# V of the first three quads loaded in two transfers, their PV evicted in two copies, and two FFN1 products placed behind the third PV

## The chip, the cores and the metric

The kernel runs on one core of one Trainium2 chip. The metric is the time of one execution on the device, in microseconds. All kernels here are one program for one core, with the inputs in HBM as float32 and the output as float32.

## What is computed

A sigmoid attention is followed by a SwiGLU feed-forward block without residuals or norms. The attention has 8 batches, 12 heads, sequence length 448 and head dimension 64; the block takes the 3584 tokens of 768 features that come out of it, with 1536 hidden features.

```python
scores = scale * np.matmul(q, k.transpose(0, 1, 3, 2)) - np.log(S)   # scale = 1/sqrt(64)
attn = 1.0 / (1.0 + np.exp(-scores))
attn_out = np.matmul(attn, v)                                        # (8, 12, 448, 64)
x = attn_out.transpose(0, 2, 1, 3).reshape(B * S, H * D)             # (3584, 768)
g = x @ w_gate
silu = g * (1.0 / (1.0 + np.exp(-g)))
out = (silu * (x @ w_val)) @ w_out                                   # (3584, 768)
```

## The kernel before

**Units of work.** The heads are taken in quads: quad `n` is the four heads `4j` to `4j+3` of batch `b`, with `n = 3b + j`, so there are 24. The 448 keys of a quad are cut into 7 chunks of 64; chunk `c` of quad `n` is written (n,c) below. For each chunk, `qk_tile` (L246) makes the scores of the four heads with four matmuls of 64 rows and 64 columns of the array (L254). They go into one PSUM tile of two banks: `h2` is the bank, and within a bank one head lies on partitions 0 to 63 and another on 64 to 127. `sig_tile` (L263) turns the tile into probabilities with one ScalarE activation of 128x896 (L273), or in two halves (L270). When the 7 chunks are there, `pv` (L276) accumulates the products with V in another PSUM tile, with 28 matmuls of 64x64 (L289), and evicts it into two SBUF tiles `xT` of 128 partitions: the features of two heads each, which is the layout that the feed-forward part reads. `trans_pe` (L235) transposes q and k of a quad on TensorE (L223, copied out by DVE at L229); later quads are transposed by DMA (L211).

**Which head lies where.** A matmul of 64 rows in the upper half of the array can write partitions of the lower half. The function `flip(n)` (L186) chooses between two layouts. Without the flip, V arrives in one transfer of 128 partitions (L197), and PV leaves the heads of bank 1 with the two partition halves exchanged, so the second eviction is two copies of 64 partitions each (L313 on DVE; for `how=2` at L311 on ScalarE), each to the other half. With the flip, V arrives in two transfers of 64 partitions (L195), which put heads 0 and 3 on one half and heads 1 and 2 on the other, the scores of the second bank are written to exchanged halves (`g` at L253), and the second eviction is one copy of 128 partitions. In the kernel before, quads 0 to 4 are not flipped and quads 5 to 23 are.

**PSUM.** All eight banks are a ring of four two-bank tiles (`ring`, L72). `Banked` (L79) takes the next tile, or the one named with `at`. A tile can be written again when its last readers are done. Thus QK waits for the sigmoid that read the tile four places earlier, and PV and the first products of FFN1 wait in the same way for their tiles.

**The order of the work.** Each engine works through its own list of instructions in order. For the first 30 us this list is written out by hand (L811 to L945): loads and casts, the chunks of quads 0, 1 and 2, their PV, and between them the transposes of the next quad and the first products of FFN1 for batch 0. In this stretch the tiles go round so that `pv(1)` takes the tile of `pv(0)`, and `early[0]`, the first FFN1 tile, takes that of `pv(1)`. From L964 on a planner mixes the attention of later quads into the feed-forward work by due times.

**FFN1.** For hidden block `f` (128 features) of batch `b`, `ffn1_mm` (L325) accumulates x times the gate weights in bank 0 and x times the value weights in bank 1, over six blocks `pr` of 128 features of x (L330). Block `pr` needs tile `xT` of quad `pr // 2`. So the first four products of a bank can run when quads 0 and 1 are evicted; products 4 and 5 wait for quad 2. In the hand-written part the first three hidden blocks (`early[0]` to `early[2]`) are begun with the first four products, around the last chunks and the PV of quad 2, and then finished.

**Queues.** q and k of quads 0 to 3 are issued by SyncE (SP; one part of quad 0's q by ScalarE), in the kernel's first microseconds. V, the weights and q and k of quads 4 to 6 are issued by GpSimd (POOL), in the order V0, V1, first gate and value weights (`wg`, `wv`), V2, second `wg` and `wv`, q and k of quad 4, q and k of quad 5, third `wg` and `wv`, V3. Each of these transfers also converts to 16 bits, except those of q and k. A POOL transfer waits at its issue for the landing of the eighth POOL transfer before it.

Of the kernel before, what the change touches and what calls it, by code (L numbers as in the profile page):

```python
# [20 lines left out]
def kernel(  # L21
# [95 lines left out]
    def apart(second, *firsts):  # L117

        for first in firsts:
            keys[0] += 1  # L120
            tc.add_to_no_dep_group(f"half{keys[0]}", first.ins)
            tc.declare_no_dep(second.ins, group=f"half{keys[0]}", reason="another bank or other partitions")
# [25 lines left out]
    def half_of(a):  # L148
        return a.rearrange("p a b s -> p (a b s)").bitcast(FP16)
# [34 lines left out]
        qkv_st[(n, which)] = st  # L184

    def flip(n):  # L186
        return n > 4

    def load_v(n):
        t = v16p.tile([128, 2, S], FP16, tag="v16", name=f"v16_{n}")  # L190
        if flip(n):
            b, j = divmod(n, NJ)
            src = v[b, 4 * j:4 * j + 4].rearrange("h (p c) d -> p h (c d)", c=C)
            for w, heads in enumerate((slice(0, 4, 3), slice(1, 3))):
                nc.gpsimd.dma_start(out=t[w * 64:(w + 1) * 64], in_=src[:, heads])  # L195
        else:
            nc.gpsimd.dma_start(out=t, in_=src_of(n, 2))  # L197
        v16[n] = t
# [47 lines left out]
    def qk_tile(n, c, at=None):  # L246
        sd = Banked(at=at)
        sc = sd.t
        qt, kt = qT[(n, 0)], qT[(n, 1, c)]
        for w in range(2):  # L250
            for h2 in range(2):
                r = slice(h2 * 64, h2 * 64 + 64)
                g = (w ^ (h2 and flip(n))) * 64  # L253
                nc.tensor.matmul(  # L254
                    out=sc[g:g + 64, h2, :S],
                    lhsT=kt[r, w * 64:(w + 1) * 64],
                    rhs=qt[r, :, w * 64:(w + 1) * 64],
                    start=True,
                    stop=True,
                )  # L260
        return sd
# [14 lines left out]
    def pv(n, how=0, at=None, then=None):  # L276

        b, j = divmod(n, NJ)
        P = Banked(at=at).t
        vt = v16.pop(n)  # L280
        for c in range(C):
            pt = pts.pop((n, c))
            for h2 in range(2):
                for w in range(2):
                    r, g = w * 64, (w ^ h2) * 64
                    if flip(n):
                        r, g = g, r
                    r = slice(r, r + 64)
                    nc.tensor.matmul(  # L289
                        out=P[g:g + 64, h2, :S],  # L290
                        lhsT=vt[r, h2, c * D:(c + 1) * D],
                        rhs=pt[r, h2, :],
                        start=(c == 0),
                        stop=(c == C - 1),
                    )

        def x_tile(h2):
            if n >= NQ - NJ:
                at = 4 * W2 + (2 * j + h2) * S
                return half_of(stg_a)[:, at:at + S]  # L300
            return xtp.tile([128, S], FP16, tag="xT", name=f"xT_{b}_{2 * j + h2}")

        xs = [x_tile(h2) for h2 in range(2)]
        first = nc.vector.tensor_copy(out=xs[0], in_=P[:, 0, :S])  # L304
        pairs = [(xs[1], P[:, 1, :S])] if flip(n) else [
            (xs[1][w * 64:(w + 1) * 64, :], P[(1 - w) * 64:(2 - w) * 64, 1, :S]) for w in range(2)
        ]
        def second():
            for o, i in pairs:
                if how == 2:  # L310
                    apart(nc.scalar.copy(out=o, in_=i), first)  # L311
                else:
                    nc.vector.tensor_copy(out=o, in_=i)  # L313

        if then is None:
            second()
        else:
            then.append(second)
        for h2 in range(2):
            xT[(b, 2 * j + h2)] = xs[h2]  # L320
# [4 lines left out]
    def ffn1_mm(D, b, f, prs, banks=(0, 1)):  # L325
        cs = slice((f % FW) * 128, (f % FW) * 128 + 128)
        for i in banks:
            for pr in prs:
                D.write(
                    nc.tensor.matmul(  # L330
                        out=D.t[:, i, :S], lhsT=(wg16, wv16)[i][f // FW][:, pr, cs], rhs=xT[(b, pr)],
                        start=(pr == 0), stop=(pr == NP - 1),
                    ),
                    i,
                )
# [447 lines left out]
    for grp in visits:  # L783
        n, c = grp[0]
# [143 lines left out]
    four = range(NP - 2)  # L928
    chunk(2, 4, at=(k0 + 1) % 4)
    early = [tile_of(0), tile_of(2)]  # L930
# [2 lines left out]
    ffn1_mm(early[0], 0, 0, (3,), (0,))  # L933
    chunk(2, 6, at=(k0 + 1) % 4)
    ffn1_mm(early[0], 0, 0, four, (1,))
    ffn1_mm(early[1], 0, 1, four, (0,))
    pv(2, how=2, at=(k0 + 3) % 4)
    ffn1_mm(early[1], 0, 1, four, (1,))
    early.append(tile_of(1))
    ffn1_mm(early[2], 0, 2, four)  # L940
# [115 lines left out]
```

## Time and profile before

| | |
|---|---|
| Median of 4 runs | 400.1 us (399.67 to 401.1) |
| The profiled execution | 399.98 us, span 397.9 us |
| TensorE (PE) busy | 387.3 us, 97% of the span |
| ScalarE (ACT) busy | 237.3 us, 60% |
| VectorE (DVE) busy | 251.1 us, 63% |
| GpSimd (POOL) busy | 124.4 us, 31% |
| Granted TensorE clock | 1.000 |

The span runs from the first to the last instruction of the profiled execution; the execution's own time also holds what lies around it. Line numbers, such as L313, are those of the kernel. In the rows, `ps_D` is any tile of the PSUM ring, `pt_a` the probabilities, `xT` the evicted attention output, `T` and `Tk` the transposed q and k, `c` the casts of q and k, `v` V, and `wg` and `wv` the gate and value weights. PEld is TensorE's weight load, which runs beside its matmuls. A row of the timeline gives start, duration, engine, line, operation, output <- inputs with their shapes, the count, and in brackets the idle time before it with what ended it. A matmul's shown duration holds its pipeline, so two that follow each other overlap in the rows. In rows of groups the figures after the count are the busy time, the mean duration of one in ns, and the idle time before.

### The profile page before, as it was taken

The page shows a single profiled execution, that of the slowest core. Times are in us where ns is not written, and L with a number is a line of the kernel's source. Part 1 is how long each engine was busy: PE and PEld are TensorE (multiplying, and loading weights), DVE is VectorE, ACT ScalarE, POOL GpSimd, SP SyncE. Part 2 cuts the span into 40 slices and gives each one's busy share as a digit, 9 for nine tenths or more (in the row PEclk, how much of TensorE's full clock was granted, in tenths as well). Part 3 has the DMA queues.
Part 4 walks back from the last instruction along what each step waited for, and adds up shares of the span by engine and source line. Part 5 has one row for each costly group of instructions (what it writes and reads, how often), then busy time and mean ns, then how long its engine had stood idle before and what let it go on. Part 6 is the DMA issues. An engine that isn't in the chain of part 4 may idle for free.

```text
span 397.9 us, 8117 instructions
## 1 busy us (share of the span) xinstructions
PE 387.3 (97%) x3110; PEld 202.2 (51%) x3110; DVE 251.1 (63%) x504; ACT 237.3 (60%) x385; POOL 124.4 (31%) x204
## 2 busy tenths in 40 slices
PE   6799999999999999999999999999999999999995
PEld 3444545444554444444455555455556655555663
DVE  3637646688643444466674564799986558787553
ACT  5956785746466787779772567866653065656000
POOL 4528141513311342343336538600007400000900
PEclk9999999999999999999999999999999999999999
DMA  8999989999599777797778697000000520000055
GB/s 260 256 250 247 238 161 232 192 172 137 140 281 232 175 165 163 163 186 164 165 163 192 107 298 159 3 2 1 1 2 0 160 79 2 2 2 0 2 171 146
DMA packets 65590, 54.39 MB, mean 137 GB/s; under 512 B 36048, under 2 KB 61744, under 8 KB 65552
## 3 DMA queue, kind: packets, MB, share of 16 engines
q1 hardware_dynamic: 49264, 36.97, 36.6%
q0 software_dynamic: 15376, 15.34, 24.4%
q10 hardware_dynamic: 912, 1.57, 1.2%
q8 instruction: 24, 0.39, 0.4%
q14 instruction: 14, 0.11, 0.1%
HBM read 47.19 MB, written 11.01 MB: 146 GB/s over the span
## 4 chain that ended last, share of the span: by engine, by line
PE 91%; DMA 2%; ACT 2%; DVE 2%; issue 1%; SPq 0%; POOL 0%; DVEq 0%; POOLq 0%
PE ps_D L330 29%; PE ps_D L639 24%; PE ps_D L466 22%; PE ps_D L254 8%; PE ps_D L289 8%; ACT pt_a L273 2%; DMA T<-c 1%; DMA st<-in_k_dram 1%; PE ps_D L223 1%; DVE xT L313 0%; DVE xT L304 0%; POOL c L204 0%; DVE T L229 0%; SPq L166 0%; SPq L211 0%
## 5 line engine op out<-in xcount | busy, mean ns | idle before, releaser
L273 ACT ACTIVATE pt_a<-ps_D 128x896 f16<-128x896 f32 x148 | 127.0, 921 | 40.8 <-PE ps_D L254 39.3
L330 PE MATMUL ps_D<-xT,wg 128*128 128x448 f16 x312 | 69.0, 353 | 0.4 <-DVE xT L313 0.3
L330 PE MATMUL ps_D<-xT,wv 128*128 128x448 f16 x312 | 68.5, 353 | 0.0
L355 DVE TENSOR_TENSOR t<-ps_D,s 128x448 f16<-128x448 f32 x52 | 32.4, 624 | 54.7 <-ACT s L353 54.3
L476 ACT ACTIVATE snap<-ps_D 128x448 f32<-128x448 f32 x66 | 34.4, 542 | 29.2 <-PE ps_D L466 28.4
L254 PE MATMUL ps_D<-T,T 64*64 64x448 bf16 x644 | 44.6, 357 | 1.6 <-ACT pt_a L273 0.7
L330 PEld LDWEIGHTS <-wg 128*128 128x128 f16 x312 | 27.9, 98 | 33.9 <-issue 11.8
L330 PEld LDWEIGHTS <-wv 128*128 128x128 f16 x312 | 30.4, 98 | 28.7 <-issue 0.6
L353 ACT ACTIVATE s<-ps_D 128x448 f16<-128x448 f32 x52 | 28.7, 551 | 22.6 <-PE ps_D L330 22.6
L639 PEld LDWEIGHTS <-S 128*128 128x128 f16 x312 | 30.2, 98 | 21.1 <-issue 1.4
L204 POOL CAST c<-stg_a 128x896 bf16<-128x896 f32 x40 | 36.5, 940 | 13.1 <-DMA stg_a<-in_q_dram 11.8
L639 PE MATMUL ps_D<-ramp_a,S 128*128 128x384 f16 x234 | 40.5, 326 | 0.0
L289 PE MATMUL ps_D<-pt_a,v 64*64 64x448 f16 x672 | 36.0, 349 | 0.8 <-ACT pt_a L273 0.4
L359 DVE SCALAR_TENSOR_TENSOR hT<-ps_D,t 128x448 f16<-128x448 f32 x52 | 32.5, 625 | 5.4
L657 DVE SCALAR_TENSOR_TENSOR osb<-ps_D,osb 128x384 f32<-128x384 f32 x40 | 22.3, 557 | 18.9 <-PE ps_D L639 16.6
L868 POOL CAST held<-S 128x1 bf16<-128x1 f16 x3 | 0.6, 191 | 104.8 <-ACT osb L650 55.7
L652 DVE TENSOR_SCALAR osb<-ps_D 128x384 f32<-128x384 f32 x37 | 20.6, 557 | 19.0 <-PE ps_D L639 16.2
L639 PEld LDWEIGHTS <-hT 128*128 128x128 f16 x228 | 22.0, 98 | 15.9 <-issue 1.6
L466 PE MATMUL ps_D<-xS,wv 128*128 128x448 f16 x132 | 28.6, 352 | 0.0
L868 POOL CAST held<-pt_a 128x1 bf16<-128x1 f16 x13 | 2.5, 192 | 82.2 <-ACT pt_a L273 82.2
L254 PEld LDWEIGHTS <-T 64*64 64x64 bf16 x644 | 15.6, 105 | 24.2 <-issue 17.6
L466 PE MATMUL ps_D<-xT,wg 128*128 128x448 f16 x132 | 26.8, 353 | 0.0
(109 smaller groups left out, 498.0 us busy)
## 6 DMA issues: line engine op xcount, KB each, us to landing
out_dram<-osb SPq DMA_DIRECT2D x45, 192.0 KB, 3.9
stg_a<-in_q_dram SPq DMA_DIRECT2D x18, 448.0 KB, 5.3
stg_a<-in_k_dram SPq DMA_DIRECT2D x18, 448.0 KB, 6.5
v<-in_v_dram POOLq DMA_DIRECT2D x38, 112.0 KB, 4.5
wg<-in_moe_w_gate_dram POOLq DMA_DIRECT2D x4, 576.0 KB, 12.6
wv<-in_moe_w_val_dram POOLq DMA_DIRECT2D x4, 576.0 KB, 14.2
wo<-in_moe_w_out_dram POOLq DMA_DIRECT2D x4, 576.0 KB, 8.8
stg_a<-in_q_dram POOLq DMA_DIRECT2D x3, 448.0 KB, 13.7
```

The source lines that it names most:

```text
L204: eng.tensor_copy(out=t.rearrange("p c h d -> p h c d"), in_=st.rearrange("p h (c d) -> p h c d", c=C))
L254: nc.tensor.matmul(out=sc[g:g + 64, h2, :S], lhsT=kt[r, w * 64:(w + 1) * 64], rhs=qt[r, :, w * 64:(w + 1) * 64], start=True, stop=True,)
L273: nc.scalar.activation(out=pt, in_=sc[:, :, :S], func=SIGM, bias=sbias, scale=qkscale)
L289: nc.tensor.matmul(out=P[g:g + 64, h2, :S], lhsT=vt[r, h2, c * D:(c + 1) * D], rhs=pt[r, h2, :], start=(c == 0), stop=(c == C - 1),)
L330: nc.tensor.matmul(out=D.t[:, i, :S], lhsT=(wg16, wv16)[i][f // FW][:, pr, cs], rhs=xT[(b, pr)], start=(pr == 0), stop=(pr == NP - 1),),
L353: D.read(nc.scalar.activation(out=s16, in_=D.t[:, 0, :S], func=SIGM), 0)
L355: D.read(nc.vector.tensor_tensor(out=t1, in0=D.t[:, 0, :S], in1=s16, op=MULT), 0)
L359: nc.vector.scalar_tensor_tensor(out=hT[(b // 2, f)][:, b % 2, :], in0=D.t[:, 1, :S], scalar=hsc(b // 2), in1=t1, op0=MULT, op1=MULT),
L466: nc.tensor.matmul(out=D.t[:, bank, :S], lhsT=W(f, j), rhs=X(j), start=(start and j == 0), stop=(stop and j == JT - 1), skip_group_check=True,
L476: D.read(nc.scalar.mul(out=o, in_=D.t[:, bank, :S], mul=scale), bank)
L639: nc.tensor.matmul(out=D.t[:, bank, :hw], lhsT=l, rhs=B_(i), start=(first and i == order[0]), stop=(i == order[-1]), skip_group_check=True,),
L657: D.read(nc.vector.scalar_tensor_tensor(out=o, in0=i, scalar=1.0 / hsc(pb), in1=o, op0=MULT, op1=ADD), bank)
```

## The change

V of quads 0, 1 and 2 takes the flipped layout: it is loaded with two transfers of 64 partitions each, the scores of these quads are written to the exchanged halves in bank 1, and each second eviction is one copy of 128 partitions, on DVE for quads 0 and 1 and on ScalarE for quad 2. Quads 3 and 4 stay as they are, with one transfer of V and three copies in all. Of the four gate products of the second hidden block that stand ahead of the PV of quad 2, the last two are placed behind it.

```diff
     def flip(n):
-        return n > 4
+        return n not in (3, 4)
...
     chunk(2, 6, at=(k0 + 1) % 4)
     ffn1_mm(early[0], 0, 0, four, (1,))
-    ffn1_mm(early[1], 0, 1, four, (0,))
+    ffn1_mm(early[1], 0, 1, range(2), (0,))
     pv(2, how=2, at=(k0 + 3) % 4)
+    ffn1_mm(early[1], 0, 1, range(2, 4), (0,))
     ffn1_mm(early[1], 0, 1, four, (1,))
     early.append(tile_of(1))
     ffn1_mm(early[2], 0, 2, four)
```

On each engine the number of compute instructions that differs is small: DVE has two copies less and ScalarE one, POOL has three DMA issues more, and TensorE's list has the same instructions in another order.

## The prediction

> **What bounds the kernel now.** I read the page's first and fourth parts, then the busy time by stretches, then the chain of waits and the timeline of the first 30 us, where the change lies, and last the landing times of the early transfers.
>
> ```profile
> PE 387.3 (97%) x3110; PEld 202.2 (51%) x3110; DVE 251.1 (63%) x504; ACT 237.3 (60%) x385; POOL 124.4 (31%) x204
> PE 91%; DMA 2%; ACT 2%; DVE 2%; issue 1%; SPq 0%; POOL 0%; DVEq 0%; POOLq 0%
> ```
>
> TensorE is the bound over the whole. Only what shortens its stream, or an idle time in it, can move the end. The stretches (columns: length, busy time of PE, PEld, DVE, ACT, POOL, granted clock, DMA share, GB/s) tell where that idle time is:
>
> ```profile
> 12.00:18.00 6.00, 4.80 (x74) 2.63 (x73) 3.38 (x6) 6.00 (x8) 2.77 (x4) 1.00 1.22 258
> 18.00:22.00 4.00, 3.34 (x55) 2.22 (x55) 3.49 (x7) 3.52 (x5) 1.45 (x2) 1.00 1.31 203
> 22.00:30.00 8.00, 8.00 (x67) 3.72 (x66) 1.66 (x4) 4.31 (x7) 1.67 (x2) 1.00 1.25 264
> 22.00:119.00 97.00, 96.94 (x826) 49.50 (x825) 60.39 (x122) 61.26 (x94) 32.40 (x49) 1.00 1.04 206
> ```
>
> ScalarE is full from 12 to 18 us (the sigmoids bound this stretch), has holes from 18 to 22, and from 22 us TensorE is full. So a gain must be made before about 23 us and must then survive. The chain of waits through that place:
>
> ```profile
> 17.01 0.63 DVE xT L313
> 17.65 0.63 DVE xT L313
> 18.28 0.04 issue
> 18.32 1.54 PE ps_D L289 x28
> ...
> 21.16 0.63 DVE xT L313
> 21.79 0.04 issue
> 21.83 0.73 PE ps_D L330 x3
> ```
>
> The second eviction of quad 0's PV is two 64-partition copies on DVE, and the PV of quad 1 (18.32) waits for their end, because it takes the same PSUM tile. The second eviction of quad 1 is again two copies, and FFN1's first product (21.83) waits for them. What this does to ScalarE, from the timeline:
>
> ```profile
> 8.50 11.45 ACT L273 ACTIVATE pt_a<-ps_D 128x896 f16<-128x896 f32 x14 [0.32 <-PE ps_D L254]
> 20.14 0.92 ACT L273 ACTIVATE pt_a<-ps_D 128x896 f16<-128x896 f32 x1 [0.20 <-PE ps_D L254]
> 21.34 3.37 ACT L273 ACTIVATE pt_a<-ps_D 128x896 f16<-128x896 f32 x4 [0.28 <-PE ps_D L254]
> ```
>
> Fourteen sigmoids run back to back, then two holes, both waiting for QK products that stand behind quad 1's PV in TensorE's order.
>
> **The change part by part.** *Copies removed.* Durations by form on DVE:
>
> ```profile
> L313 DVE CAST xT<-ps_D 128x448 f16<-128x448 f32 x16 | 9.8, 613 | 0.0
> L313 DVE CAST xT<-ps_D 64x448 f16<-64x448 f32 x8 | 5.0, 622 | 0.2
> ```
>
> A copy of 64 partitions takes as long as one of 128. One copy less each for quads 0 and 1 saves about 0.63 us of DVE each; for quad 2 it saves one of two 526 ns copies on ScalarE.
>
> *Quad 0.* The second eviction ends at 17.01 + 0.61 = 17.62 instead of 18.27. PV(1) is next limited by TensorE itself: the QK of chunk (2,1) starts at 17.56 and a 64-row product follows another after 0.18, so PV(1) starts at about 17.75 instead of 18.32: 0.57 earlier. Its last operand, the sigmoid of (1,6), ends at 18.32 and is needed at 17.75 + 1.13 = 18.88; V of quad 1 is also there (see below). Everything behind PV(1) moves by 0.57: QK(2,2) from 19.64 to 19.07, the transposes of quad 3 from 19.96 to 19.39 (their casts on DVE also end 0.65 earlier, at 18.8), QK(2,3) from 20.85 to 20.28.
>
> *ScalarE behind it.* The sigmoids' pitch in the run is 0.80, so (2,2) starts at 18.94 + 0.80 = 19.74 instead of 20.14, limited by ScalarE; (2,3) can start 0.50 after its QK, at 20.78 instead of 21.34 (0.50 is QK to sigmoid in the trace: 19.64 to 20.14 and 20.85 to 21.34). The hole of 0.20 is gone, that of 0.28 shrinks. (2,4), whose sigmoid follows at 0.81, ends at 22.50 instead of 23.07.
>
> *Quad 1.* Its evictions end at 20.57 instead of 21.78 (0.57 from the start, 0.64 from the copy). FFN1's first product is then late by TensorE alone: QK(2,4) waits for the sigmoid of (2,2), whose tile it takes, to about 20.79, and the product comes 0.31 behind it, at 21.10 instead of 21.83. This 0.73 is not kept: the QK of (2,6) needs the tile of (2,4), free at 22.50, so it starts at 22.54 instead of 23.12. **That is the gain that lasts: 0.57 to 0.58 us**, from where on TensorE has no wait.
>
> *Two products moved.* Two FFN1 products of 0.19 leave the row before PV(2) and join the row behind it. Sum on TensorE: nothing, and no switch between row shapes more. PV(2) starts 0.57 + 0.38 earlier, at 24.10 instead of 25.05. It is covered: its tile is free when (2,5) ends (23.3), and the last sigmoid (2,6) ends at 24.1 and is needed at 25.25. The evictions of quad 2 (0.62 on DVE beside 0.53 on ScalarE) have the products between PV(2) and 28.2 over them, 2.65 us, so what they save is worth nothing here. Without that cover it would be 0.53.
>
> *V in halves: the cost.* Three DMA issues more on POOL: 0.60 twice (1.22 for a pair in the timeline) for one of 0.72 to 0.88, so +0.35 to +0.5 per quad. After V0 POOL waits for quad 1's q anyway (7.58), which hides it. After V1 the issues of the first FFN weights and of V2 come 0.5 to 0.7 later. Each POOL transfer also waits for the landing of the eighth before it, and with more transfers these are others: the second weight pair waits for V0's halves (to about 13 instead of 11.5), quad 4's q and k for V1's halves, quad 5's k for the first wv (22.2 instead of 20.0). What is queued behind them is more of the same queue, and that queue works in order with a backlog of 10 us and more, so none of these arrives later; from V3 on the waits fall on the same transfers as before. SP's queue and ScalarE's issues are not touched; bytes and packets are the same.
>
> What must be in time is V0. Landings, us after the issue (the rows of the issues at 4.73, 8.46, 10.01, 10.82 and of a pair at 57.61, which also runs beside loads of SP's queue):
>
> ```profile
> v<-in_v_dram POOLq DMA_DIRECT2D x1, 224.0 KB, 8.1
> v<-in_v_dram POOLq DMA_DIRECT2D x1, 224.0 KB, 7.3
> wv<-in_moe_w_val_dram POOLq DMA_DIRECT2D x1, 576.0 KB, 12.2
> v<-in_v_dram POOLq DMA_DIRECT2D x1, 224.0 KB, 12.6
> v<-in_v_dram POOLq DMA_DIRECT2D x1, 112.0 KB, 6.6
> v<-in_v_dram POOLq DMA_DIRECT2D x1, 112.0 KB, 6.8
> ```
>
> V0 lands at 12.9 and PV(0) starts at 13.51, released by a sigmoid (13.46), so 0.6 is spare. The pair landed 6.6 and, issued 0.57 later, 6.8 + 0.57 = 7.4 after the first issue. Bounds: V0 0.8 earlier to 0.1 later than now, by that row. The Trainium skill, "DMA: Bandwidth & Descriptors", section "Rules for kernel authors", speaks against this change: two transfers to disjoint partition halves serialize, so one of 128 partitions is to be used; its section "Anatomy of one DMA — SWDGE (gpsimd) path" gives each transfer a fixed cost of some 2.0 us. By the page V0's second half lands at about 14.9, PV(0) starts 1.4 late, and as QK(1,5) (16.04, right behind the transposes that follow PV(0)) and its sigmoid (0.50 later, 16.53) have nothing spare, all of it reaches the end: -0.57 + 1.4 = +0.8. By the trace's rows the fixed part of the second transfer overlaps the first, and the sum stays -0.57. I take the trace, and keep +0.8 as the far end. An earlier V0 would take bandwidth from quad 1's k (8.72, cast at 8.74); its first sigmoid has about 0.7 spare, so I cost that at nothing. Of the others, V1 lands at 15.7 against 17.75, the first wv at 22.2 against 22.86 (0.6 spare, before 1.2), V2 at 23.4 against 24.10 (0.7 spare, before 1.7).
>
> **Sum.** -0.57 us against the profiled execution (span 397.9, its time 399.98, so 2.1 lie outside the span): 399.4. The median of the four runs is 400.1, 0.1 above it; 0.57 off that is 399.5.
>
> **The rivals.**
> - *V0's halves come late* (the case that ends slower). One mechanism: the second half pays its start behind the first. From a slip of 0.6 PV(0) waits, from 1.2 the gain is eaten, from 2.4 the kernel is slower by 0.3%. With 2.0 it gives 400.9. For it: the skill's rule, and that V0 is the first transfer of its queue beside a full SP queue. Against: the pair at 57.61.
> - *The new spare times are too small.* If issues that are 0.5 to 0.7 later push the first wv or V2 beyond 22.9 or 24.1, or if ScalarE's pitch does not hold, the 0.57 turns into a wait for DMA in FFN1's first products: 399.9 to 400.2. For it: both spares fall to 0.6 and 0.7. Against: the queue is never empty from 12.6 us on, so the order of landings is set by bytes.
> - *More is gained*: the 0.73 at FFN1's first product is kept, if (2,6) does not wait for its tile, or quad 1 starts earlier too. 399.2 at best; TensorE's idle time from 12 to 22 us is 1.86 in all and most of it belongs to ScalarE's sigmoids.
> - *The move does nothing*, as costed; it is not told apart from the rest by the time.
>
> **How the numbers follow.** The forecast 0.60, late halves 0.17, spare times too small 0.15, more gained 0.08. The median of the runs can tell about 0.3%, 1.2 us (the four runs lie 1.4 apart), from no change, so the forecast itself counts as no change. Faster by over 0.3% needs under 398.9: the two gaining cases and a low draw of the runs, 0.14. Slower needs over 401.3: the late halves beyond their 2.0, or with a high draw, 0.13. Between is 0.73. Range: 0.57 gained with the runs' scatter of 0.7 below, up to 400.9 of the late halves.
>
> **What would show it.** Right: one 128-partition copy at L313 for quads 0 and 1, PV(1) near 17.75 released by no DVE copy, ScalarE without the hole of 0.20, PV(2) near 24.1, and the same products from 30 us on about 0.57 earlier. The step "V0 in time" is wrong if PV(0) or its weight load is released by a DMA after 13.5. "Spares" is wrong if L330 or PV(2) waits for wv or v. The forecast as a whole is wrong if the start of the stage at 258 us (an unbroken row of L466) does not move by the gain at 30 us, or if QK or PV products take another time with the heads' halves exchanged.

## The result and the profile after

The changed kernel takes 399.57 us (median of 34 runs, 399.01 to 401.56), the kernel before 400.31 us (55 runs, 399.47 to 401.9). The ratio is 0.9982, with a 95% interval of 0.9975 to 0.9990: 0.7 us gained, 0.4 to 1.0 by the interval. The whole spread of the runs moved with it: the fastest runs lie 0.5 us apart, the lower and the upper quarter points 0.7. The forecast was 0.57 us of gain and 399.5 us; against the median of 400.31 that gain makes 399.7. The change is smaller than the 0.3% that the prediction took as the least that its runs could show, but over this many runs it is distinct from nothing.

The page of the profiled execution, however, shows a longer span than before, 398.6 against 397.9 us (its own time was 400.33 us). Its busy times, its chain and its granted clock by slices:

```profile
PE 389.2 (98%) x3110; PEld 203.0 (51%) x3110; DVE 249.6 (63%) x502; ACT 236.7 (59%) x384; POOL 125.6 (32%) x207
PEclk8799999999999999999999999999999999999998
...
PE 84%; DVE 6%; ACT 4%; DMA 3%; issue 1%; SPq 0%; POOL 0%; ACTq 0%; DVEq 0%; POOLq 0%
```

TensorE is still the bound; the DVE share of the chain comes from a later stage (from 259 us), where the walk back runs beside TensorE's unbroken row. What is new is the clock: the first two of the 40 slices have 0.8 and 0.7. By stretches (length, busy time of PE, PEld, DVE, ACT, POOL, clock, DMA share, GB/s):

```profile
6.00:12.00 6.00, 4.36 (x43) 2.42 (x35) 2.23 (x4) 4.31 (x6) 3.95 (x7) 0.61 1.08 345
12.00:18.00 6.00, 5.42 (x79) 2.95 (x79) 4.17 (x8) 6.00 (x8) 4.19 (x6) 0.82 1.23 254
18.00:22.00 4.00, 3.71 (x66) 2.27 (x62) 3.26 (x7) 3.98 (x6) 0.72 (x1) 1.00 1.30 203
22.00:30.00 8.00, 7.92 (x69) 3.74 (x66) 1.08 (x2) 3.86 (x6) 2.40 (x3) 1.00 1.24 266
```

From 6 to 18 us the clock was 0.61 and 0.82; in the profile of before it was 1.00. Read from the span's start, this execution hides the change. So the stretch that the change bears on is read from its own start. It is called the ramp here: from the start of the long run of sigmoids, chunk (0,2), to the end of the last, (2,6). In the kernel before it is 8.50 to 24.71, 16.21 us. In the timeline of the profile after:

```profile
9.42 15.63 ACT L273 ACTIVATE pt_a<-ps_D 128x896 f16<-128x896 f32 x19 [1.40 <-PE ps_D L254]
17.82 0.61 DVE L313 CAST xT<-ps_D 128x448 f16<-128x448 f32 x1
18.68 1.52 PE L289 MATMUL ps_D<-pt_a,v 64*64 64x448 f16 x28
```

The run starts 0.92 us late: the last part of quad 0's k landed at 6.83 instead of 6.38, before the first transfer of V moved a byte, and the transposes behind it ran at the halved clock. But all nineteen sigmoids are now one row, without the two holes of before: 15.63 us, 0.58 less. Quad 0's second eviction is one copy of 0.61, and PV(1) is not released by DVE any more. The forms of that copy on DVE:

```profile
L313 DVE CAST xT<-ps_D 128x448 f16<-128x448 f32 x18 | 11.0, 613 | 0.0
L313 DVE CAST xT<-ps_D 64x448 f16<-64x448 f32 x4 | 2.5, 622 | 0.1
```

Two copies more of the whole form, four fewer of the halves; the four left are quads 3 and 4. V of quad 0, in halves (the first issued at 4.73, the second at 5.49):

```profile
v<-in_v_dram POOLq DMA_DIRECT2D x1, 112.0 KB, 7.2
v<-in_v_dram POOLq DMA_DIRECT2D x1, 112.0 KB, 7.6
```

The second half is there 8.3 us after the first issue; the single transfer of before took 8.1. V of quad 0 is complete at 13.05, and its PV starts at 14.44.

### The profile page after: what moved, and what is told of

Same layout as the page of the kernel before. It is cut to its first block, busy times and chain, and to the rows that moved or that the text cites. A ratio compares the mean times of both kernels' runs of the same rounds, so it can differ in the third digit from the quotient of the medians.

```text
span 398.6 us, 8115 instructions
## 1 busy us (share of the span) xinstructions
PE 389.2 (98%) x3110; PEld 203.0 (51%) x3110; DVE 249.6 (63%) x502; ACT 236.7 (59%) x384; POOL 125.6 (32%) x207
## 4 chain that ended last, share of the span: by engine, by line
PE 84%; DVE 6%; ACT 4%; DMA 3%; issue 1%; SPq 0%; POOL 0%; ACTq 0%; DVEq 0%; POOLq 0%
PE ps_D L330 29%; PE ps_D L639 24%; PE ps_D L466 14%; PE ps_D L254 8%; PE ps_D L289 7%; ACT pt_a L273 3%; DMA T<-c 1%; DMA st<-in_k_dram 1%; DVE small L489 1%; DVE S L560 1%; DVE pt_a L411 1%; DVE v L506 1%; ACT snap L476 1%; PE ps_D L223 1%; DVE v L502 1%
## 5 line engine op out<-in xcount | busy, mean ns | idle before, releaser
L330 PE MATMUL ps_D<-xT,wg 128*128 128x448 f16 x312 | 69.2, 354 | 0.0
L652 DVE TENSOR_SCALAR osb<-ps_D 128x384 f32<-128x384 f32 x37 | 20.6, 557 | 19.1 <-PE ps_D L639 15.7
L639 PEld LDWEIGHTS <-hT 128*128 128x128 f16 x228 | 22.1, 98 | 15.6 <-issue 1.2
L195 POOL DMA_DIRECT2D v<-in_v_dram x44 | 26.3, 604 | 3.5 <-DMA wg<-in_moe_w_gate_dram 2.9
```

Source lines behind the costliest of these rows:

```text
L330: nc.tensor.matmul(out=D.t[:, i, :S], lhsT=(wg16, wv16)[i][f // FW][:, pr, cs], rhs=xT[(b, pr)], start=(pr == 0), stop=(pr == NP - 1),),
L639: nc.tensor.matmul(out=D.t[:, bank, :hw], lhsT=l, rhs=B_(i), start=(first and i == order[0]), stop=(i == order[-1]), skip_group_check=True,),
```

## The experiments

Each time is the median of that kernel's runs; ratios are to the kernel before, run on the same chip, with 95% intervals.

**A second profile of the changed kernel.**

> The changed kernel once more, for a second profile of it. Theory: ramp 15.6 to 15.7 whatever the clock at its start, PV of quad 1 not released by a DVE copy, time 0.4 to 1.0 us below before.

399.66 us, ratio 0.9981 (0.9966 to 0.9995). This profile had the full clock, a span of 397.3 us, and a ramp of 8.38 to 24.00, 15.62 us. From its timeline:

```profile
16.78 0.61 DVE L313 CAST xT<-ps_D 128x448 f16<-128x448 f32 x1
17.63 1.52 PE L289 MATMUL ps_D<-pt_a,v 64*64 64x448 f16 x28
21.00 0.74 PE L330 MATMUL ps_D<-xT,wg 128*128 128x448 f16 x3
22.43 0.38 PE L254 MATMUL ps_D<-T,T 64*64 64x448 bf16 x4
23.98 1.52 PE L289 MATMUL ps_D<-pt_a,v 64*64 64x448 f16 x28
```

These are PV(1), FFN1's first product, the scores of (2,6), and PV(2). Counted from the ramp's start they lie at 9.25, 12.62, 14.05 and 15.60. The prediction's 17.75, 21.10, 22.54 and 24.10, less its 8.50, are 9.25, 12.60, 14.04 and 15.60. V of quad 0 was complete at 12.73, 0.7 before its PV at 13.39.

**The layout without the moved products.**

```diff
-        return n > 4
+        return n not in (3, 4)
```

> The flipped layout, the halves of V and the single second evictions for quads 0, 1 and 2, without the two moved FFN1 products. Measure beside the time: the ramp, from the start of the long run of sigmoids (the sigmoid of chunk (0,2)) to the end of the last sigmoid of quad 2; it is 16.21 us before (8.50 to 24.71) and 15.63 in the changed kernel (9.42 to 25.05). Theory (the gain comes from quad 0's second eviction being one copy, and ends in ScalarE's run): ramp 15.6 to 15.7, time 0.5 to 0.7 us below before, like the whole change. Rival (the moved products carry part of the gain): ramp 15.9 or more, and the time less than 0.4 below before.

399.50 us, ratio 0.9980 (0.9969 to 0.9991): all of the gain. The profile's ramp, 16.03 us, missed the expected 15.6 to 15.7:

```profile
8.78 3.34 ACT L273 ACTIVATE pt_a<-ps_D 128x896 f16<-128x896 f32 x4 [0.56 <-PE ps_D L254]
12.42 12.38 ACT L273 ACTIVATE pt_a<-ps_D 128x896 f16<-128x896 f32 x15 [0.30 <-PE ps_D L254]
```

Its extra hole, 0.30 us before 12.42, is the end of a stretch with halved clock (8.7 to 12.1 us); the holes near 20 and 21 us that the change was to close are closed.

**The moved products alone.**

```diff
-    ffn1_mm(early[1], 0, 1, four, (0,))
+    ffn1_mm(early[1], 0, 1, range(2), (0,))
     pv(2, how=2, at=(k0 + 3) % 4)
+    ffn1_mm(early[1], 0, 1, range(2, 4), (0,))
```

> Only the two FFN1 products are placed behind quad 2's PV; V and the evictions as before. Theory: ramp 16.2, PV of quad 2 about 0.38 us earlier against the ramp's start, and the first product that needs quad 2's features not earlier; time equal to before within 0.2 us. Rival (the moved products carry part of the gain): 0.2 to 0.4 us below before.

400.12 us, ratio 0.9991 (0.9980 to 1.0002). The interval holds both nothing and the rival's 0.4 us, so the time leaves it open; what the profile shows is the ramp. The three rows of its run of sigmoids:

```profile
8.34 11.44 ACT L273 ACTIVATE pt_a<-ps_D 128x896 f16<-128x896 f32 x14 [0.58 <-PE ps_D L254]
19.98 0.92 ACT L273 ACTIVATE pt_a<-ps_D 128x896 f16<-128x896 f32 x1 [0.20 <-PE ps_D L254]
21.18 3.37 ACT L273 ACTIVATE pt_a<-ps_D 128x896 f16<-128x896 f32 x4 [0.28 <-PE ps_D L254]
```

The holes of 0.20 and 0.28 and the ramp of 16.21 us are those of before. PV(2) starts 0.38 earlier against the ramp's start (24.51 - 8.34 = 16.17, before 16.55). The first gate activation, which needs quad 2's features, starts at 29.20, 20.86 from the ramp's start, exactly as before (29.36 - 8.50). So the move brings nothing in this stage.

**All of the change, but the copies cut in two again.**

```diff
-        pairs = [(xs[1], P[:, 1, :S])] if flip(n) else [
+        pairs = [(xs[1], P[:, 1, :S])] if flip(n) and n > 4 else [(xs[1][w * 64:(w + 1) * 64, :], P[w * 64:(w + 1) * 64, 1, :S]) for w in range(2)] if flip(n) else [
```

> The changed kernel, with the second eviction of quads 0, 1 and 2 cut again into two copies of 64 partitions each, now straight and not exchanged; layout, halves of V and moved products stay. Theory: the copy count is all there is to the gain, so the second PV waits for DVE again, ramp 16.2, time equal to before within 0.2 us. Rival (the halves of V, the exchanged scores or the moved products carry the gain): ramp 15.6 to 15.9 and time 0.3 to 0.7 below before.

400.34 us, ratio 1.0002 (0.9989 to 1.0015): the gain is gone. PV(1) and FFN1's first product wait for the copies again:

```profile
19.71 1.52 PE L289 MATMUL ps_D<-pt_a,v 64*64 64x448 f16 x28 [0.31 <-DVE xT L313]
23.12 0.73 PE L330 MATMUL ps_D<-xT,wg 128*128 128x448 f16 x3 [0.24 <-DVE xT L313]
```

The expected ramp of 16.2 was not seen: this profile had a halved clock from 13.4 to 16.8 us and a ramp of 17.66, with two holes of 0.93 and 0.38 in that stretch and just behind it. The time and the two waits carry the verdict.

**Halves of V alone, in the old layout.**

```diff
+        elif n < 3:
+            b, j = divmod(n, NJ)
+            src = v[b, 4 * j:4 * j + 4].rearrange("h (p c) d -> p h (c d)", c=C)
+            for w in range(2):
+                nc.gpsimd.dma_start(out=t[w * 64:(w + 1) * 64], in_=src[:, w:4:2])
```

> The kernel before, with V of quads 0, 1 and 2 in two transfers of 64 partitions each but in the old layout, so three copies as before. Measures the cost of the halves alone. Theory (the second half overlaps the first): V of quad 0 complete 7.4 to 8.4 us after its first issue, ramp 16.2, time equal to before within 0.2 us. Rival (the fixed cost of a transfer is paid twice[...]): V of quad 0 complete about 10 us after its first issue, the PV of quad 0 released by a DMA, time 1.0 to 1.4 us above before.

400.26 us, ratio 1.0000 (0.9985 to 1.0016). The landings of V0's halves, issued at 4.64 and 5.40, and quad 0's PV (L294 here):

```profile
v<-in_v_dram POOLq DMA_DIRECT2D x1, 112.0 KB, 6.7
v<-in_v_dram POOLq DMA_DIRECT2D x1, 112.0 KB, 7.1
```

```profile
13.57 1.52 PE L294 MATMUL ps_D<-pt_a,v 64*64 64x448 f16 x28 [0.43 <-ACT pt_a L278]
```

V0 is complete at 12.45, 7.8 us after its first issue, and its PV is released by a sigmoid. The halves cost nothing here; the rival of a fixed cost paid twice, about 10 us, is out for this place.

**One quad alone.** Quad 0 only, then quad 1 only:

```diff
-        return n > 4
+        return n > 4 or n == 0     # the other kernel: n == 1
```

> Only quad 0 takes the new layout (one transfer pair, one second eviction); quads 1 and 2 and the products as before. Theory: quad 0's copy alone lets quad 1's PV start about 0.57 earlier, and ScalarE's run is then limited by itself, so the ramp is 15.6 to 15.7 and the time 0.5 to 0.7 below before, the whole gain. Rival (quads 0 and 1 share the gain): ramp 15.9, time about 0.3 below.

> Only quad 1 takes the new layout; quads 0 and 2 and the products as before. Theory: FFN1's first product starts up to 0.6 earlier against the ramp's start, but the scores of chunk (2,6) wait for the sigmoid of (2,4) as before, so the ramp is 16.1 to 16.2 and the time equal to before within 0.2. Rival (FFN1's start carries the gain): time 0.3 to 0.6 below before.

Quad 0: 399.70 us, ratio 0.9987 (0.9973 to 1.0001). Quad 1: 400.29 us, 1.0000 (0.9988 to 1.0013). The run of sigmoids with quad 0 only:

```profile
9.24 15.66 ACT L273 ACTIVATE pt_a<-ps_D 128x896 f16<-128x896 f32 x19 [1.41 <-PE ps_D L254]
```

One row of 15.66 us, as in the changed kernel. With quad 1 only:

```profile
17.84 1.52 PE L289 MATMUL ps_D<-pt_a,v 64*64 64x448 f16 x28 [0.38 <-DVE xT L313]
20.94 0.74 PE L330 MATMUL ps_D<-xT,wg 128*128 128x448 f16 x3
```

PV(1) still waits for quad 0's two copies. FFN1's first product starts at 20.94, 12.93 from the ramp's start instead of 13.34, and yet the ramp is 16.19: nothing behind it in the ramp can use the earlier start. The time of the first kernel alone would not settle that quad 0 has all of the gain (0.52 us, with nothing just inside its interval); the ramps do.

**V of quad 0 late, and the same with TensorE kept at work.** The later issue of V of quad 0 also puts off V of quad 1 and the first weights. The six added products are of zeros, and nothing reads them.

```diff
-    load_v(0)
     cast(1, 0, G)
+    load_v(0)
...
+    for _ in range(6):      # the second kernel only
+        nc.tensor.matmul(out=ring[ring_at[0] % 4][:, 1, :], lhsT=warm[:, :128], rhs=warm, start=True, stop=True)
     pv(0, then=then)
```

> The changed kernel with V of quad 0 issued behind the cast of quad 1's q on POOL, so about 3.7 to 4.3 us later; V of quad 1 and the first weights about 1.2 later. Doubles the suspected weak point, V of quad 0 in time. Theory: it has about 0.6 us to spare, and what is beyond goes to the end one for one: V of quad 0 lands 2.5 to 3.5 later than now, its PV waits for the DMA by 2 to 3, time 1.5 to 2.8 us above the changed kernel. Rival (a late PV of quad 0 is caught up, since ScalarE has scores ready): time less than 0.7 above the changed kernel.

> The kernel with V of quad 0 issued late, with six products of zeros (128x512, not used for the output) on TensorE in front of quad 0's PV, in the time in which it waits for V. In the run without them that PV waited 1.58 us for V, the granted clock was halved for 6.83 us from 14.02 on, and the time rose by 3.8 us. Theory (about 1.2 us of the 3.8 is the late V itself, the rest is the halved clock): clock 1.0 from 12 to 24 us and time 1.0 to 1.8 us above the changed kernel. Rival (all is the wait's own, by way of ScalarE): 3 us or more above, as without them.

The first took 403.43 us (6 runs), ratio 1.0067 (1.0043 to 1.0091): 3.4 to 3.8 us above the changed kernel, by the ratios and by the medians. That is more than either forecast had; the six runs lie between 401.76 and 404.26. Its PV(0) and the stretches around it:

```profile
14.85 3.18 PE L289 MATMUL ps_D<-pt_a,v 64*64 64x448 f16 x28 [1.58 <-DMA v<-in_v_dram]
```

```profile
12.00:14.00 2.00, 0.95 (x12) 0.35 (x11) 0.82 (x1) 2.00 (x4) 2.00 (x4) 1.00 1.22 234
14.00:16.00 2.00, 1.15 (x13) 0.57 (x17) 0.00 (x0) 1.37 (x3) 1.34 (x3) 0.50 1.24 187
16.00:18.00 2.00, 2.00 (x27) 0.90 (x19) 0.00 (x0) 0.81 (x1) 2.00 (x3) 0.50 1.31 203
```

V0 was complete at 15.16, 6.49 after the ramp's start, 1.5 later than PV(0)'s tile is free (13.46 - 8.50 = 4.96). But the clock was halved from 14.0 to 20.8 us (the fall came 0.76 us after TensorE had run out of work at 13.26), PV(0) took 3.18 instead of 1.52, and the ramp became 19.48 us, 3.86 longer. With products of zeros in the wait:

```profile
15.82 1.96 PE L289 MATMUL ps_D<-pt_a,v 64*64 64x448 f16 x28 [0.54 <-DMA v<-in_v_dram]
```

```profile
14.00:16.00 2.00, 1.41 (x6) 0.49 (x5) 0.00 (x0) 1.39 (x2) 1.07 (x2) 1.00 1.19 174
16.00:18.00 2.00, 1.93 (x34) 0.94 (x34) 0.10 (x1) 0.92 (x1) 1.94 (x3) 1.00 1.29 196
```

401.60 us, ratio 1.0028 (1.0015 to 1.0040), about 1.9 us above the changed kernel, although V0 came even later (16.22, 7.41 from the ramp's start, 2.4 too late). The ramp is 18.00 us, 2.4 longer: one for one. That is one profile, of an execution 1.4 us above the median, with a halved clock from 7.8 to 11.3 us, before the wait. The expected 1.0 to 1.8 was meant for a V0 as late as in the first kernel. The second kernel lost less with a V0 that came later, so most of what the first lost beyond its 1.5 us was the clock.

**Quads 3 and 4 in the new layout too.** `flip` returns True for every quad.

> The changed kernel with quads 3 and 4 in the new layout too (two more transfer pairs, two fewer copies). Theory: TensorE is full from 24 us on and DVE is not on the path there, so two copies less are worth nothing; time within 0.2 us of the changed kernel. Rival (the more single copies, the better): 0.3 or more below the changed kernel; or, if halves at that place of POOL's queue delay the weights behind them, 0.3 or more above.

399.62 us, ratio 0.9981 (0.9972 to 0.9990), the same as the changed kernel. Two more copies saved where TensorE has no wait show no gain. In this profile the first value weights landed at 22.83, and their first product waited for them:

```profile
22.87 0.49 PEld L330 LDWEIGHTS <-wv 128*128 128x128 f16 x4 [0.30 <-DMA wv<-in_moe_w_val_dram]
```

V2 landed at 23.98, and PV(2) behind these products started at 24.11, 15.70 from the ramp's start, 0.1 later than planned. Up to there the queue is that of the changed kernel. So the spare times of the weights and of V2, put at 0.6 and 0.7, can be used up; the ramp stayed at 15.62.

**Products of zeros in TensorE's early idle times.** Seven of them, then only the last three (`filler(k, n)` issues n such products into tile k of the ring, and nothing reads them):

```diff
+    filler(3, 2)            # the first kernel only
     chunk(0, 0)
     chunk(0, 1)
+    filler(1, 2)            # the first kernel only
+    copy_k = trans_part(Dk, 1, 0, 1, KS, C, V, dk[1])
+    filler(1, 3)
+    copy_k()
-    trans_part(Dk, 1, 0, 1, KS, C, V, dk[1])()
```

> The changed kernel with seven products of zeros (128x512, not used for the output) on TensorE in the idle times before 9 us: two before the first scores, two before the transposes of the rest of quad 0's k, three behind these. Theory (the spread of the runs comes from the clock: where TensorE is idle for long between 4 and 9 us, the granted clock is halved for 3.4 or 6.8 us): granted clock 1.0 from 6 to 18 us, ramp 15.6, median 0.1 to 0.5 us below the changed kernel, with few runs above 400.2. Rival (the added products delay the first scores by more than the clock saves): 0.1 to 0.5 above.

> The changed kernel with only three products of zeros (128x512, not used for the output) on TensorE, those behind the transposes of the rest of quad 0's k, where it waits for DVE's copy anyway (7.4 to 7.9 us). Theory (the products that stood before the first scores and before these transposes delayed them in the earlier run; these three delay nothing and make a halved clock rarer): start of the long run of sigmoids as early as in the changed kernel at full clock (8.4 us after an equally early k), median 0.1 to 0.3 us below the changed kernel. Rival (a halved clock is no more rare, or costs the median nothing): equal to the changed kernel within 0.1.

Seven: 399.64 us, ratio 0.9988 (0.9976 to 0.9999), no gain over the changed kernel. The clock was 1.00, but the ramp started at 9.30 instead of 8.38 after a k that landed equally early: the products stood before the scores and the transposes and delayed them, as the rival said. Three: 399.36 us, ratio 0.9976 (0.9965 to 0.9986), the lowest of all, and the ramp started at 8.51. Its interval overlaps that of the changed kernel, and its own profile had a halved clock from 13.6 to 17.0 us, so that it is faster than the changed kernel, and why, stays open.

## Why the prediction was right, and where not

*Copies and PV(1).* Right. A copy of half the partitions costs as much as one of all (622 and 613 ns), and it was quad 0's second one that held PV(1): cut again, the gain is gone; with quad 0 alone, ScalarE's run is as short as with all.

*ScalarE behind it.* Right, to 0.02 us at the four places read. The holes of 0.20 and 0.28 closed, and at the end of the ramp the gain is what ScalarE's run lost, 0.58 us.

*Behind the ramp.* Not as written. The start of the stage at 258 us was to move by the same 0.57. Its first row, before and in the second profile of the changed kernel:

```profile
258.10 2.44 PE L466 MATMUL ps_D<-xT,wg 128*128 128x448 f16 x12
257.02 2.44 PE L466 MATMUL ps_D<-xT,wg 128*128 128x448 f16 x12
```

From the ramp's start these are 249.60 and 248.64, and 248.83 in the changed kernel's first profile: 0.96 and 0.77 earlier instead of 0.57. From there to the end of the span the changed kernel took 140.3 us instead of 139.8, so 0.5 was lost again. Of what was gained behind the ramp, 0.25 is a wait of TensorE at 120.9 us; only the four kernels with two copies for each of quads 0 to 2 have it. Of what was lost, 0.2 is a wait at 288.8 us, and 0.3 lies behind the last product. The profiles name no releaser for either wait. The kernel with the halves alone has the longer last stage too (140.3), and the interval of its time, 0.6 us either way, does not rule that out as a cost of the halves. So it is in part luck that the whole came out near the forecast: two differences that the forecast did not have are of opposite sign. Their causes stay open.

*Quad 1.* Right: FFN1's first product came 0.72 earlier against the ramp's start, and this was not kept beyond the scores of (2,6). That the tile freed by the sigmoid of (2,4) holds these scores follows from the tile order and fits 14.05 against 14.04; it was not tested by another tile order.

*The moved products.* Costed at nothing, and the profile of the move alone shows nothing.

*Halves.* Right to take the trace. The rule of the Trainium skill ("DMA: Bandwidth & Descriptors", "Rules for kernel authors": one 128-partition transfer rather than two halves) stood behind the far end of +0.8, an estimate in which the halves cost 1.4; the halves alone cost 0.0 by the time. The second half landed 1.2 and 1.1 us after the first in the two profiles whose landings are shown, not the 2.0 that the estimate added to a whole transfer.

*Spare times.* V of quad 0 was in time in both profiles of the changed kernel. That the weights' 0.6 is thin shows in the kernel with all quads in halves, where it was used up.

*Late V0, the rival's price.* The mechanism is real, but the term "all of it reaches the end", one for one, was mis-sized. It fits the one profile that had the full clock from the wait on (2.4 too late, ramp 2.4 longer). As it would happen, with TensorE idle in the wait, 1.5 too late cost 3.9 of ramp in the one profile of it. The prediction should have weighed the clock here. The Trainium skill ("TensorE: Matmul & The Clock Gate", Part 1 on the HAM clock gate) has the rule that an idle window of about 3.4 us brings the clock to one half. By its letter it would not have given this fall, which came 0.76 us into a wait of 1.58; the measurement decides, and the last section has what the traces say of it. V of quad 0 came 2.1 later there than in the kernel before, from the ramp's start, and the kernel was slower by 0.67%. So the point at which late halves make it slower by 0.3% lies nearer than the slip of 2.4 that the prediction named.

*The size.* 0.57 was forecast, 0.7 measured with 0.4 to 1.0 in the interval; the remaining 0.1 to 0.2 is not resolved. Single profiles can't settle it: from the ramp's start to the end of the span those of the changed kernel are 0.26 and 0.46 shorter than before, and those of three kernels without gain (the move, the halves, quad 1) 0.1 to 0.4 longer.

## What to carry to other kernels

A copy of half the partitions took as long here as one of all (622 and 613 ns), so two cost twice one; choose the layout upstream so that the eviction is one copy, first where a PSUM tile is waited for. Follow a gain through every later wait before counting it: here 0.63 of copy became 0.57 at PV(1), 0.72 at FFN1, and 0.58 at the end of the ramp, while the same copy saved in quad 1, and in quads 3 and 4, showed no gain (quad 2 was not tried alone). Then look past the stage: small waits far behind it moved too. And where a stage's start drifts from run to run, compare stages from their own start.

## What the runs showed of the hardware

The granted clock of TensorE was halved for 3.41 or 6.83 us, once or twice the same length, somewhere between 7 and 21 us in 8 of the 14 profiles of this case, of kernels that differ little. The two profiles of the changed kernel, with and without it, differ by 1.2 us of span, more than the change brings; a k that landed 0.57 later is part of that. The stage leaves TensorE idle in short pieces: in the profile of before it was busy 3.72 of the 6 us from 6 to 12 and kept its clock.

These busy times hold the pipeline of the matmuls, so the limit can't be read from them. A count made afterwards narrows it. Cut each profile into stretches of 3.41 us from the moment at which its clock is first full, up to 30 us. Count each product only for the time that its columns take, 0.19 us for 448 (the pitch of FFN1's products in the rows) and others in proportion, with overlapping ones once. Then TensorE had filled at most 0.38 of the stretch just ahead of each of the eight falls, and at least 0.40 of each of the 88 stretches after which the clock stayed full. In the kernel with V of quad 0 late that stretch was 0.27 full; with the products of zeros, the stretch ahead of PV(0) was 0.48. The kernel before is near the edge itself, with 0.41 in the stretch from 5.21 us. It is a fit to these profiles; no kernel was run to try it.
